# Backward pass of a cached-attention block: Wo times dao in batches, and another order of the first heads' work and transfers

## The chip, the cores and the metric

The kernel runs on one core of a Trainium2 chip. The metric is the device time of one execution in microseconds, given as the median of several runs. Engines are named as the profile names them: PE is TensorE (PEld its weight loads), DVE is VectorE, ACT is ScalarE, POOL is GpSimd, SP is SyncE, which here only issues DMAs.

## What is computed

A block with one query token (D = 640) and a cached attention of 32 heads, 8192 keys, head width 192, then a small mixer and MLP; the reference returns the output and the gradients of nine inputs. What matters here is the attention and its backward pass:

```python
q = (x @ wq)                       # 32 heads of 192
scores = einsum('bhqd,bhkd->bhqk', q, k) * Dh ** (-0.5)
p = softmax(scores)
o = einsum('bhqk,bhkd->bhqd', p, v)
a = o.reshape(B, Sq, Hq * Dh) @ wo
...
_out, _vjp = jax.vjp(_f, A_x, A_k_cache, A_v_cache, A_wq, A_wo, B_w3, B_w4, c, w_mod)
_grads = _vjp(grad_out)
```

For each head the backward pass needs, with dao the gradient of a (640 numbers) and P the softmax row: do = Wo·dao (192 numbers), dV = P ⊗ do, dP = V·do, c = do·o, dS = P·(dP - c), dK = dS ⊗ q, and dq from sums that the forward pass kept. K, V, dK and dV are each 100 MB in bf16 and go through HBM once, so 400 MB of the 569 MB that the kernel moves are these four.

## The kernel before

**Layout.** A head's K or V is 8192 rows of 192; a tile holds half a head, 128 partitions by 32 rows by 192 (128 x 6144 bf16, 1536 KB). Five such tiles ("big") serve the outputs dV and dK in the backward pass; six more slots (three in a pool "fv", three in "bv") form a ring for V.

**Order.** The forward pass takes heads 0 to 31 (to about 545 us), then the small mixer and its backward pass (to about 566 us), then the backward pass of the heads runs from 31 down to 0. The loop index i counts them: head HS[i] = 31 - i, and "nxt" is the head of i + 1. Iteration i computes dP, dS and dK of head i, and dV of head i + 1, so dV runs one head ahead. The first V tiles, both dV halves of head i = 0 and the first half of i = 1 are made ahead of the loop.

**One iteration of the loop** (lines 1235 to 1284), in program order:

1. On odd i, `bwd_dob` (L979): broadcasts do and q of the next pair of heads over all partitions, by matmuls with the identity (L191) that ScalarE copies out as do_pb and q_pb (L195).
2. `bwd_mult` (L996) for both halves t: VectorE multiplies V by do in place (`mul`, L132), and TensorE sums the product over groups of 8 columns into dP_ps by 24 accumulating matmuls (L1004). This frees the V slot.
3. `ring_load` (L749): issues the next transfers whose slot is free. A ring entry is half a V ("v", on SP's queue, L330) or a batch of Wo ("w", on POOL's queue, L764).
4. `bwd_pf` and `bwd_dv` (L1023) of the next head: ScalarE scales the first 20 rows of each half (L1009, one instruction a row), VectorE makes the other 12 (L987), and SP stores the half (L1012), which waits for both.
5. `hook` (L1188), in the first ten iterations: do of heads further on. Wo arrives as 15 pairs of heads in batches of three pairs (the last has two), one batch for two iterations. `bwd_ttr` (L920) multiplies one 640-wide row block of Wo by the broadcast dao and sums it, on VectorE, five and four blocks in the two iterations; then `fin_do`, `fin_c` (c = do·o, its sum on TensorE, L145) and `fin_dq_mm` (dq's matmuls, L950 to L953).
6. Store jobs: dwo (three ScalarE copies, L1054, stored from POOL's queue, L1073) and others.
7. `bwd_ds` (L1028): dP's last sum (L1030) and dS. For i = 0 then `dq_last` (L958), 128 small matmuls with K (L493, L496).
8. `bwd_dk` (L1035) for both halves: one VectorE product (L987) and one store on SP (L1039).

**What sets the order.** PE, DVE and ACT run in program order (`pin_order` at the end). SP and POOL carry only DMAs, in an order that the framework's scheduler gives them; each queue issues in that order, and an entry that waits holds those behind it. All big transfers, loads and stores, are on SP's queue.

The change touches `load_wo` (L761), `hook` (L1188), the tables ahead of it (L1176 to L1185) and the loop, and adds `bwd_wo_mult` and `bwd_wo_red` beside `bwd_ttr`.

Of the kernel before, what the change touches and what calls it, by code (L numbers as in the profile page):

```python
# [12 lines left out]
AX = mybir.AxisListType  # L13
# [7 lines left out]
def kernel(  # L21
# [43 lines left out]
    P = 128  # L65
# [62 lines left out]
    def ccol(n, name, dtype=FP32):  # L128
        return const.tile([P, n], dtype, name=name)

    def mul(out, a, b):
        nc.vector.tensor_tensor(out=out, in0=a, in1=b, op=ALU.mult)  # L132
# [600 lines left out]
    PS = list(range(HH - 1, -1, -1))  # L733
    V_b = {HS[0]: st[HS[0]]["V"], HS[1]: {1: st[HS[1]]["V"][1]}}
    wo_src = {(PS[k], cc): st[2 * PS[k] + 1]["wo"][:, cc, :] for k in range(2) for cc in range(3)}
    BATCHES = [(2, 3, 4), (5, 6, 7), (8, 9, 10), (11, 12, 13), (14, 15)]
    ring = []
    for i in range(1, HQ):
# [10 lines left out]
    def ring_load():  # L749
        while ring_n[0] < len(ring) and (ring_n[0] < 3 or ring_key(ring_n[0] - NR) in freed):  # L750
            n = ring_n[0]
            kind, k, t = ring[n]
            slot = ring_slot(n)
            pool = bv if slot > 2 else fv
            ring_n[0] += 1
            if kind == "v":
                V_b.setdefault(k, {})[t] = load_v(pool, k, t, slot, ldq if n >= 3 else nc.sync)
            else:
                load_wo(k, pool.tile([P, JH, DH], BF16, name="V_sb", tag=f"v{slot}"))

    def load_wo(k, tl):  # L761
        lo, n = PS[BATCHES[k][-1]], len(BATCHES[k])
        tl = tl.rearrange("p j d -> p (j d)")[:, 0 : 3 * n * D].rearrange("p (c r) -> p c r", r=D)
        nc.gpsimd.dma_start(out=tl, in_=wo_v[:, 3 * lo : 3 * (lo + n), :])  # L764
        for hp in range(lo, lo + n):
            for cc in range(3):
                wo_src[hp, cc] = tl[:, 3 * (hp - lo) + cc, :]

    def ring_key(n):
        return ring[n] if n >= 0 else (("v", HS[0], 0), ("v", HS[0], 1), ("v", HS[1], 1))[n]  # L770
# [144 lines left out]
    dmod_bf = ccol(NMC, "dmod_bf", BF16)  # L915

    dof = ccol(NQC, "dof")
    r3_all = ccol(NQC, "r3_all")

    def bwd_ttr(hp, cc):  # L920
        nc.vector.tensor_tensor_reduce(out=wo_src[hp, cc], in0=wo_src[hp, cc], in1=dao_bc, scale=1.0, scalar=0.0, op0=ALU.mult, op1=ALU.add, accum_out=dof[:, 3 * hp + cc : 3 * hp + cc + 1])  # L921

    def fin_do(lo, n):
        sl = slice(3 * lo, 3 * (lo + n))
        dve_copy(do_bf[:, sl], dof[:, sl])

    def fin_c(lo, n):
        sl = slice(3 * lo, 3 * (lo + n))
        dve_copy(do_f[:, sl], do_bf[:, sl])
        pc = bsm.tile([P, 9], FP32, name="pc")[:, 0 : 3 * n]  # L930
        mul(pc, do_f[:, sl], o_col_f[:, sl])
        pc2 = bsm.tile([P, 6], FP32, name="pc2")[:, 0 : 2 * n]
        stt(pc2[:, 0 : 2 * n : 2], pc[:, 1 : 3 * n : 3], mask_lo[:, 0:1], pc[:, 0 : 3 * n : 3], ALU.mult, ALU.add)
        stt(pc2[:, 1 : 2 * n : 2], pc[:, 1 : 3 * n : 3], mask_hi[:, 0:1], pc[:, 2 : 3 * n : 3], ALU.mult, ALU.add)
        return col_sums(pc2, 2 * n, "c_ps")
# [87 lines left out]
    def bwd_dv(h, t):  # L1023
        o = big_tile("dV")
        bwd_dv_act(o, h, t)
        bwd_dv_dve(o, h, t)
# [146 lines left out]
    J2[NPH + 8].append(job_x0)  # L1173
    J2[NPH + 14].append(job_c)

    ttrs = {i: [] for i in range(NPH)}  # L1176
    ttrs[0] = [(PS[1], cc) for cc in range(3)]
    fins = {}
    for b, ks in enumerate(BATCHES):
        units = [(PS[k], cc) for k in ks for cc in range(3)]  # L1180
        i = 1 + 2 * b
        ttrs[i] = units[0:5] if i + 1 < NPH else units
        if i + 1 < NPH:
            ttrs[i + 1] = units[5:]
        fins[min(i + 1, NPH - 1)] = (PS[ks[-1]], len(ks), b)  # L1185
    dq, cps = {}, {}

    def hook(i):  # L1188
        for u in ttrs[i]:
            bwd_ttr(*u)  # L1190
        if i == 0:
            fin_do(PS[1], 1)
            cps[i] = (PS[1], 1, fin_c(PS[1], 1))
        if i in fins:
            lo, n, b = fins[i]
            if b > 0:
                freed.add(("w", b, 0))
                ring_load()
            fin_do(lo, n)
            cps[i] = (lo, n, fin_c(lo, n))  # L1200
            dq[i] = (lo, n, fin_dq_mm(lo, n))
        if i == 3:
            dq[i] = (PS[1], 2, fin_dq_mm(PS[1], 2))
# [28 lines left out]
    bcast_dao()  # L1232
    mid_mm()
    AHEAD = 2 * NPH
    for i in range(HQ):
        h, nxt = HS[i], HS[i + 1] if i + 1 < HQ else None
        if i % 2 == 1 and nxt is not None:
            bwd_dob(nxt // 2)
        for f in J0[i]:
            f()  # L1240
        if i <= AHEAD:
            for t in range(2):
                bwd_mult(h, t, 2 if i == 0 else 1)
                if i == t == 0:
                    ring_load()
                    c_first = fin_c(PS[0], 1)
        ring_load()
        if i - 1 in dq:
            fin_dq(*dq.pop(i - 1))
        if i == 0:  # L1250
            fin_c_copy(PS[0], 1, c_first)
        if nxt is not None:
            if i > 0:
                bwd_pf(nxt)
            for t in range(0 if i > 0 else 1, 2):
                bwd_dv(nxt, t)
        if i < NPH:
            hook(i)
        if i == 3:
            bcast_cols(du_bf, 0, NFC, du_bc, act_copy)  # L1260
        for f in J1[i]:
            f()
        bwd_ds(h)
        if i == 0:
            dq_last(h)
        if i >= AHEAD and nxt is not None:
            for t in range(2):
                bwd_mult(nxt, t)
        bwd_dk(h, 0)
        bwd_dk(h, 1)  # L1270
        if i in cps:
            fin_c_copy(*cps.pop(i))
        if i == 1:
            mid_cols()
            job_mid()
            dve_copy(dmod_bf[:, 2 * NDC : 6 * NDC], dmod_c[:, 2 * NDC : 6 * NDC])
        if i == NPH - 1:
            fin_dq(*dq.pop(i))
            mm_cm.__exit__(None, None, None)
            for nm, b in (("in", 1), ("out", 4), ("bc", 1)):  # L1280
                side_cm.append(tc.tile_pool(name="side" + nm, bufs=b, side="right", reuse_waits="tile"))
                side[nm] = side_cm[-1].__enter__()
        for f in J2[i]:
            f()
        if i == I_SIDE:
            while side_cm:
                side_cm.pop().__exit__(None, None, None)
            xt = ctx.enter_context(tc.tile_pool(name="xt", bufs=1, side="right", reuse_waits="tile"))
            for k in "xy":
                tail_tiles[k] = (xt, "xt" + k)  # L1290
            for n in range(len(ring) - NR, len(ring)):
# [34 lines left out]
```

## Time and profile before

| | |
|---|---|
| median of 3 runs | 1381.43 us (1379.37 to 1382.59) |
| profiled execution | 1379.59 us, of which the span of instructions is 1377.8 us |
| DVE busy | 1070.5 us (78%) |
| ACT busy | 946.8 us (69%) |
| PE busy | 860.8 us (62%) |
| DMA | 569.26 MB, mean 413 GB/s; SP's queue 550.73 MB, POOL's 16.71 MB |
| V load (125 of them) | 1536 KB, 14.8 us from issue to landing (median) |
| dV store (61) and dK store (64) | 1536 KB each, 22.3 and 24.0 us |

How to read it: an engine's busy share is a mean over stages with different limits. "DMA share" is the mean busy share of the core's 16 DMA engines, so one engine alone is 0.06; it can read slightly over 1 because packets overlap by a few nanoseconds. "PEclk" is the granted share of TensorE's clock. In the view of stretches each row has the stretch, its length, then busy time and count of instructions for each engine, then the granted clock, the DMA share and the rate in GB/s. A row of the timeline has the start, the time, the engine, the line, the operation and the count of instructions merged into it.

### The profile page before, as it was taken

How to read it: one execution, taken by the hardware profiler on the slowest of the kernel's cores; microseconds unless marked ns; L12 is line 12 of the kernel's file. 1: busy time of each engine (PE TensorE's matmuls, PEld its weight loads, DVE VectorE, ACT ScalarE, POOL GpSimd, SP SyncE). 2: the span in 40 equal slices, each digit the busy share in tenths (PEclk: the TensorE clock that was granted, in tenths of full speed). 3: DMA queues.
4: the chain of work that ended last, by engine and by line, in shares of the span. 5: the costliest groups of instructions: out<-in, count | busy, mean ns of one | idle time of the engine just before them, and what ended most of it. 6: DMA issues, size and time to landing. Idle time of an engine off the chain costs nothing.

```text
span 1377.8 us, 28365 instructions
## 1 busy us (share of the span) xinstructions
PE 860.8 (62%) x11655; PEld 675.9 (49%) x11655; DVE 1070.5 (78%) x1273; ACT 946.8 (69%) x2586; POOL 21.5 (2%) x33
## 2 busy tenths in 40 slices
PE   3799999999999999748545653443344325324440
PEld 3577777777777777736434542322223223213330
DVE  3588787888788787899988986965868669679792
ACT  1388777887778785866676676766767676767770
POOL 0000000000000000000000000000000000000000
PEclk9899999999999999666666665666666767656665
DMA  9999999999999999899999999999999999999997
GB/s 392 416 417 418 420 418 421 414 419 418 405 421 419 403 420 387 337 367 413 419 418 419 427 429 425 425 427 423 426 426 423 428 422 415 425 425 422 428 428 319
DMA packets 71758, 569.26 MB, mean 413 GB/s; under 512 B 6796, under 2 KB 14476, under 8 KB 31436
## 3 DMA queue, kind: packets, MB, share of 16 engines
q1 hardware_dynamic: 67934, 550.73, 96.1%
q0 software_dynamic: 3664, 16.71, 3.0%
q8 instruction: 91, 1.49, 0.4%
q14 instruction: 39, 0.32, 0.1%
q10 hardware_dynamic: 30, 0.00, 0.0%
HBM read 341.51 MB, written 225.91 MB: 412 GB/s over the span
## 4 chain that ended last, share of the span: by engine, by line
DMA 37%; DVE 29%; PE 22%; ACT 6%; SPq 3%; issue 2%; DVEq 0%; ACTq 0%
DMA out_dram<-dV 24%; DVE prod L132 9%; PE ps_a L432 8%; DVE dK L987 5%; DVE V_sb L132 5%; DMA out_dram<-dK 4%; PE S_ps L372 4%; DMA V_sb<-in_A_v_cache_dram 3%; DMA K_sb<-in_A_k_cache_dram 3%; ACT dV L1009 3%; PE ps_b L443 3%; PE kb_ps L449 2%; DVE dV L987 2%; DVE V_sb L921 2%; DMA out_dram<-dw 2%
## 5 line engine op out<-in xcount | busy, mean ns | idle before, releaser
L1009 ACT ACTIVATE dV<-do_pb,PF 128x192 bf16<-128x192 bf16 x1246 | 435.8, 440 | 141.9 <-DMA out_dram<-dV 101.3
L1004 PE MATMUL dP_ps<-V_sb,ident_bf 128*128 128x256 bf16 (+1 forms) x1584 | 233.3, 322 | 212.0 <-DVE V_sb L132 212.0
L407 ACT ACTIVATE EK<-K_sb,E_f 128x192 bf16<-128x192 bf16 x992 | 351.1, 442 | 4.3 <-PE kb_ps L302 2.9
L1004 PEld LDWEIGHTS <-ident_bf 128*128 128x128 bf16 x1584 | 180.9, 117 | 264.2 <-issue 138.9
L987 DVE TENSOR_TENSOR dK<-dS,q_pb 128x6144 bf16<-128x6144 bf16 x64 | 212.9, 3354 | 26.2 <-DMA out_dram<-dK 15.6
L132 DVE TENSOR_TENSOR prod<-K_sb,q_pb 128x6144 bf16<-128x6144 bf16 x64 | 214.4, 3349 | 4.1 <-DMA K_sb<-in_A_k_cache_dram 4.1
L132 DVE TENSOR_TENSOR V_sb<-V_sb,do_pb 128x6144 bf16<-128x6144 bf16 (+1 forms) x66 | 212.0, 3253 | 0.0
L432 PE MATMUL ps_a<-EK,V_sb 128*128 128x193 bf16 x1984 | 195.1, 251 | 1.3 <-DMA V_sb<-in_A_v_cache_dram 1.3
L432 PEld LDWEIGHTS <-V_sb 128*128 128x128 bf16 x1984 | 167.8, 100 | 19.3 <-issue 12.7
L987 DVE TENSOR_TENSOR dV<-P2h,do_pb 128x2304 bf16<-128x2304 bf16 (+2 forms) x67 | 89.5, 1354 | 111.3 <-DMA out_dram<-dV 106.8
L414 DVE TENSOR_TENSOR EK<-K_sb,P2h 128x1536 bf16<-128x1536 bf16 x124 | 117.5, 948 | 0.0
L372 PE MATMUL S_ps<-prod,ident_bf 64*64 64x256 bf16 x3072 | 101.3, 280 | 11.5 <-DVE prod L132 11.5
L443 PE MATMUL ps_b<-EK,V_sb 128*64 128x193 bf16 x1984 | 107.7, 250 | 0.0
L372 PEld LDWEIGHTS <-ident_bf 64*64 64x64 bf16 x3072 | 86.5, 110 | 31.0 <-issue 26.9
L443 PEld LDWEIGHTS <-V_sb 128*64 128x64 bf16 x1984 | 80.8, 110 | 19.6 <-issue 15.9
L393 ACT ACTIVATE E_f<-sm_ps,negm 128x64 f32<-128x64 f32 x31 | 9.8, 315 | 103.9 <-DVE negm L391 103.9
L376 DVE TENSOR_REDUCE S<-S_ps 128x128 f32<-128x1024 f32 x32 | 39.2, 1224 | 47.7 <-PE S_ps L372 47.6
L1115 PEld LDWEIGHTS <-ident_bf 128*128 128x128 bf16 x112 | 15.2, 136 | 123.8 <-issue 122.9
L449 PE MATMUL kb_ps<-EK,hot_bf 128*32 128x384 bf16 x992 | 63.5, 333 | 0.0
L1115 PE MATMUL js_ps<-wq,ident_bf 128*128 128x480 bf16 x64 | 23.8, 557 | 53.3 <-DVE wq L132 53.3
L1115 PE MATMUL js_ps<-wm,ident_bf 128*128 128x400 bf16 x48 | 14.9, 494 | 48.7 <-DVE wm L132 48.7
L195 ACT CAST do_pb<-bc_ps 128x384 bf16<-128x384 f32 x15 | 7.1, 474 | 52.0 <-PE bc_ps L191 52.0
(259 smaller groups left out, 758.5 us busy)
## 6 DMA issues: line engine op xcount, KB each, us to landing
V_sb<-in_A_v_cache_dram SPq DMA_DIRECT2D x125, 1536.0 KB, 14.8
K_sb<-in_A_k_cache_dram SPq DMA_DIRECT2D x64, 1536.0 KB, 14.2
out_dram<-dK SPq DMA_DIRECT2D x64, 1536.0 KB, 24.0
out_dram<-dV SPq DMA_DIRECT2D x61, 1536.0 KB, 22.3
wq<-in_A_wq_dram SPq DMA_DIRECT2D x3, 2560.0 KB, 31.4
wo_t<-in_A_wo_dram SPq DMA_DIRECT2D x16, 480.0 KB, 14.3
out_dram<-dwo POOLq DMA_DIRECT2D x16, 480.0 KB, 8.9
wq<-in_A_wq_dram SPq DMA_DIRECT2D x4, 1920.0 KB, 23.7
```

The source lines that it names most:

```text
L132: nc.vector.tensor_tensor(out=out, in0=a, in1=b, op=ALU.mult)
L372: nc.tensor.matmul(st["S_ps"][c0 : c0 + 64, r, t * JH : (t + 1) * JH, :], lhsT=ident_bf[64 * r : 64 * r + 64, 64 * r : 64 * r + 64], rhs=p ...
L376: nc.vector.reduce_sum(out=st["S2"], in_=st["S_ps"], axis=AX.X)
L407: nc.scalar.activation(out=st["EK"][q][:, jj, 0:DH], in_=K_st[h, t][:, r * JQ + jj, :], func=ACT.Copy, scale=st["E_f"][:, j : j + 1])
L414: nc.vector.tensor_tensor(out=EK[:, NA:JQ, 0:DH].rearrange("p j (d r) -> p j d r", r=2), in0=K_st[h, t][:, r * JQ + NA : (r + 1) * JQ, :]. ...
L432: nc.tensor.matmul(st["A_ps"][:, 0:n], lhsT=V_sb[:, r * JQ + jj, a0:a1], rhs=EK[:, jj, 0:n], start=(q == 0 and jj == 0), stop=(q == 3 and ...
L443: nc.tensor.matmul(st["B_ps"][g : g + 64, 0:n], lhsT=V_sb[:, r * JQ + jj, b0:b1], rhs=EK[:, jj, 0:n], start=(q == 0 and jj < 2), stop=(q = ...
L449: nc.tensor.matmul(kb_ps[g : g + 32, 0 : 2 * DH], lhsT=hot_bf[:, HQ - 1 - h : 2 * HQ - 1 - h], rhs=EK[:, jj : jj + 2, 0:DH], start=(h == 0 ...
L987: nc.vector.tensor_tensor(out=o.rearrange("p j (d r) -> p j d r", r=2), in0=pairs[:, :, None, :].to_broadcast([P, n, NP2, 2]), in1=vec.rea ...
L1004: nc.tensor.matmul(bst[h]["dP_ps"][:, t * JH + r : t * JH + r + n, :], lhsT=ident_bf, rhs=V_sb[:, :, k * DS : (k + 1) * DS], start=(k == 0 ...
L1009: nc.scalar.activation(out=o[:, jj, :], in_=vec_of(do_pb, h), func=ACT.Copy, scale=bst[h]["PF"][:, t * JH + jj : t * JH + jj + 1])
L1115: nc.tensor.matmul(ps[:, 0 : NDC * W].rearrange("p (i w) -> p i w", w=W), lhsT=ident_bf, rhs=w[:, :, k * W : (k + 1) * W], start=(k == 0), ...
```

## The change

Four things, all in the first ten iterations of the loop:

- Wo times dao by batches: one product over a whole batch on VectorE (9 x 640 columns; 6 x 640 for the last) in odd iterations, whose sums TensorE takes by 20 accumulating matmuls with the identity into 32 columns a block; one VectorE reduction in the next iteration (the same one for the last batch) gives do.
- `bwd_dob` moves into the hook for i up to 8: behind `fin_do`, ahead of `fin_c` and of dq's matmuls. For i = 0, `bwd_ds` and `dq_last` go ahead of the hook.
- For i = 1 to 3, `bwd_pf` goes ahead of the V products and each dV half behind the V product of the same t.
- For i = 0 to 3, the second `ring_load` goes behind `bwd_dv`.

On the engines' queues this gives the following. SP, from the first V load of the loop on: before, V V dV dK dK, V dV dV dK dK, V V dV dV dK dK, V dV dV dK dK, dV dV V V V dK dK; after, V dV V dK dK, dV dV V dK dK, dV dV V V dK dK, dV dV V V dK dK, V V dV dV dK dK. On POOL the Wo load of the second batch stands behind the first store of dwo, before it stood ahead. PE gets 100 matmuls more; DVE loses 42 products with their 42 reads of the accumulator, and gets five products and five reductions.

```diff
+    def bwd_wo_mult(b):
+        lo, n = PS[BATCHES[b][-1]], len(BATCHES[b])
+        w = wo_b.pop(b)
+        mul(w, w, dao_bc[:, None, :].to_broadcast([P, 3 * n, D]))
+        ps = bank_s("dof_ps")[:, 0 : 3 * n * WS].rearrange("p (c w) -> p c w", w=WS)
+        for k in range(D // WS):
+            nc.tensor.matmul(ps, lhsT=ident_bf, rhs=w[:, :, k * WS : (k + 1) * WS], start=(k == 0), stop=(k == D // WS - 1))
+        dof_ps[b] = (ps, lo, n)
+
+    def bwd_wo_red(b):
+        ps, lo, n = dof_ps.pop(b)
+        nc.vector.reduce_sum(out=dof[:, 3 * lo : 3 * (lo + n)], in_=ps, axis=AX.X)
...
     def hook(i):
-        for u in ttrs[i]:
-            bwd_ttr(*u)
         if i == 0:
+            for u in wo_first:
+                bwd_ttr(*u)
             fin_do(PS[1], 1)
+            bwd_dob(PS[1])
             cps[i] = (PS[1], 1, fin_c(PS[1], 1))
-        if i in fins:
-            lo, n, b = fins[i]
+            return
+        if i % 2 == 1:
+            b = (i - 1) // 2
+            bwd_wo_mult(b)
             if b > 0:
                 freed.add(("w", b, 0))
                 ring_load()
+        if i in fins:
+            b = fins[i]
+            lo, n = PS[BATCHES[b][-1]], len(BATCHES[b])
+            bwd_wo_red(b)
             fin_do(lo, n)
+            if i % 2 == 0:
+                bwd_dob(HS[i + 2] // 2)
             cps[i] = (lo, n, fin_c(lo, n))
             dq[i] = (lo, n, fin_dq_mm(lo, n))
...
+    EARLY, SPLIT = range(4), range(1, 4)
     for i in range(HQ):
         h, nxt = HS[i], HS[i + 1] if i + 1 < HQ else None
-        if i % 2 == 1 and nxt is not None:
+        if i % 2 == 1 and i > NPH and nxt is not None:
             bwd_dob(nxt // 2)
...
         if i <= AHEAD:
+            if i in SPLIT:
+                bwd_pf(nxt)
             for t in range(2):
                 bwd_mult(h, t, 2 if i == 0 else 1)
                 if i == t == 0:
                     ring_load()
                     c_first = fin_c(PS[0], 1)
-        ring_load()
+                if i in SPLIT:
+                    bwd_dv(nxt, t)
+        if i not in EARLY:
+            ring_load()
...
-        if nxt is not None:
+        if nxt is not None and i not in SPLIT:
             if i > 0:
                 bwd_pf(nxt)
             for t in range(0 if i > 0 else 1, 2):
                 bwd_dv(nxt, t)
+        if i in EARLY:
+            ring_load()
+        if i == 0:
+            bwd_ds(h)
+            dq_last(h)
         if i < NPH:
             hook(i)
...
-        bwd_ds(h)
-        if i == 0:
-            dq_last(h)
+        if i > 0:
+            bwd_ds(h)
```

More of the change, by code (lines that the diff above doesn't have):

```diff
@@ L735 @@
     wo_src = {(PS[k], cc): st[2 * PS[k] + 1]["wo"][:, cc, :] for k in range(2) for cc in range(3)}
+    wo_b = {}
+    WS = 32
     BATCHES = [(2, 3, 4), (5, 6, 7), (8, 9, 10), (11, 12, 13), (14, 15)]
@@ L763, in load_wo @@
         tl = tl.rearrange("p j d -> p (j d)")[:, 0 : 3 * n * D].rearrange("p (c r) -> p c r", r=D)
+        wo_b[k] = tl
         nc.gpsimd.dma_start(out=tl, in_=wo_v[:, 3 * lo : 3 * (lo + n), :])
-        for hp in range(lo, lo + n):
-            for cc in range(3):
-                wo_src[hp, cc] = tl[:, 3 * (hp - lo) + cc, :]
     def ring_key(n):
@@ L917 @@
     dof = ccol(NQC, "dof")
+    dof_ps = {}
     r3_all = ccol(NQC, "r3_all")
@@ L1174 @@
     J2[NPH + 14].append(job_c)
[L1176 to L1185, printed above, removed]
+    wo_first = [(PS[1], cc) for cc in range(3)]
+    fins = {min(2 + 2 * b, NPH - 1): b for b in range(len(BATCHES))}
     dq, cps = {}, {}
     def hook(i):
-        for u in ttrs[i]:
-            bwd_ttr(*u)
         if i == 0:
+            for u in wo_first:
+                bwd_ttr(*u)
             fin_do(PS[1], 1)
+            bwd_dob(PS[1])
             cps[i] = (PS[1], 1, fin_c(PS[1], 1))
-        if i in fins:
-            lo, n, b = fins[i]
+            return
+        if i % 2 == 1:
+            b = (i - 1) // 2
+            bwd_wo_mult(b)
             if b > 0:
```

## The prediction

> **What bounds the kernel now.** First the page: the strip of DMA shares and rates, and the chain of work that ended last.
>
> ```profile
> span 1377.8 us, 28365 instructions
> ...
> DMA  9999999999999999899999999999999999999997
> GB/s 392 416 417 418 420 418 421 414 419 418 405 421 419 403 420 387 337 367 413 419 418 419 427 429 425 425 427 423 426 426 423 428 422 415 425 425 422 428 428 319
> ...
> DMA 37%; DVE 29%; PE 22%; ACT 6%; SPq 3%; issue 2%; DVEq 0%; ACTq 0%
> ```
>
> A slice is 34.4 us. The sixteen DMA engines move above 400 GB/s nearly everywhere; slices 16 to 18 (516 to 620 us) drop to 387, 337, 367. The change touches only what starts at 575 us. So I cut that region into short stretches (the view of busy time by stretches; the last two columns are DMA share and GB/s).
>
> ```profile
> core 0: us, PE busy (x) PEld busy (x) DVE busy (x) ACT busy (x) POOL busy (x), PEclk, DMA share, GB/s
> 580.00:582.00 2.00, 2.00 (x36) 2.00 (x35) 2.00 (x2) 2.00 (x7) 0.00 (x0) 0.97 0.76 300
> 582.00:584.00 2.00, 2.00 (x38) 1.98 (x36) 2.00 (x3) 2.00 (x7) 0.00 (x0) 1.00 0.83 206
> ...
> 588.00:592.00 4.00, 3.67 (x122) 3.56 (x121) 3.97 (x3) 0.00 (x0) 0.00 (x0) 0.50 1.00 329
> 592.00:602.00 10.00, 4.79 (x37) 3.42 (x35) 9.90 (x6) 8.68 (x25) 0.00 (x0) 0.50 1.01 427
> 602.00:603.00 1.00, 1.00 (x6) 0.71 (x5) 1.00 (x1) 1.00 (x4) 0.00 (x0) 0.50 0.53 221
> 603.00:604.00 1.00, 1.00 (x7) 0.73 (x5) 1.00 (x2) 1.00 (x4) 0.00 (x0) 0.50 0.14 41
> 604.00:605.00 1.00, 1.00 (x11) 0.87 (x10) 1.00 (x2) 1.00 (x4) 0.00 (x0) 0.99 0.99 160
> 605.00:606.00 1.00, 1.00 (x11) 0.90 (x10) 1.00 (x5) 1.00 (x5) 0.00 (x0) 1.00 0.43 135
> ...
> 612.00:1360.00 748.00, 325.53 (x1992) 245.59 (x1992) 593.68 (x503) 507.40 (x1318) 17.44 (x22) 0.65 1.01 424
> 1360.00:1368.00 8.00, 0.00 (x0) 0.00 (x0) 0.00 (x0) 0.00 (x0) 0.00 (x0) 0.50 0.95 404
> 1368.00:1372.00 4.00, 0.00 (x0) 0.00 (x0) 0.00 (x0) 0.00 (x0) 0.00 (x0) 0.50 0.29 123
> 1372.00:1376.00 4.00, 0.00 (x0) 0.00 (x0) 0.00 (x0) 0.00 (x0) 0.00 (x0) 0.50 0.06 28
> ```
>
> From 612 to 1360 us the share is 1.01: no engine's work there is worth anything, only bytes are. What can be won lies before 612: the hole from 602 to 606, (0.47 + 0.86 + 0.01 + 0.57) = 1.9 us by share, and by bytes against 427 GB/s (206 + 386 + 267 + 292 KB) / 427 = 2.7 us, since a queue that restarts is slow; and 580 to 584 (0.8 us by share). What was late for the hole? SP's queue, in order of time:
>
> ```profile
> 581.43 3.27 SPq L330 DMA_DIRECT2D V_sb<-in_A_v_cache_dram  x2
> 585.44 0.34 SPq L1012 DMA_DIRECT2D out_dram<-dV  x1
> 591.75 3.60 SPq L1039 DMA_DIRECT2D out_dram<-dK  x2
> 603.68 0.34 SPq L330 DMA_DIRECT2D V_sb<-in_A_v_cache_dram  x1
> 604.12 4.69 SPq L1012 DMA_DIRECT2D out_dram<-dV  x2
> ```
>
> Nothing is issued from 595.4 to 603.68. Then comes a V load, held by TensorE's last read of its slot, and behind it the first dV half of the head, although VectorE had finished that half at 603.1. A transfer is 1.57 MB, 3.7 us at 427 GB/s.
>
> **The change, part by part** (i is the loop's index, times those of this profile).
>
> *i = 0, the hole.* VectorE is unchanged up to the dV half that ends at 584.03. dP's sum, now next, waits for TensorE's last product (584.35): 0.68 + 0.35, dS at 585.45 instead of 588.3. Three Wo products (0.74 apart, 2.3) and the small do and c steps (586.38 to 587.34, 0.95) follow: 588.7. Two dK (6.63): 595.3, 0.3 later than now. dq_last's matmuls (588.38 to 592.2, 3.8) now run from 585.45 to 589.3, then the broadcasts (0.48): do_pb cast at 590.3, q_pb 590.9, PF 591.2. ScalarE starts dV at 591.2 instead of 594.5; twenty rows take 7.0: halves done at 598.2 and 605.2 instead of 601.5 and 608.5.
>
> *i = 1.* VectorE: P2h 0.2, V product 3.3, dV part 1.3: the first half is whole at 600.2 (now issued at 604.1). Product and part again: 604.85; ScalarE's 605.2 ends the second (now 608.48). Behind it, SP's V load goes at 605.6 (now 603.68) and needs nothing by then: V is used three heads later. DMA is busy with dK until about 602.7, the first half carries it to 606.4, and the second, issued at 605.2, comes 1.0 to 1.3 us later (the issue at 603.68 shows in the row from 604): 606.2 to 606.5. The hole shrinks to 0.1 at most; 0.3 is kept for it. What is late next is ScalarE's second half.
>
> *Gain:* 1.9 to 2.7 less 0.3: 1.6 to 2.4, taken at 2.0, the middle.
>
> *Price in i = 0:* the second V load now stands behind the dV store, which waits for ScalarE until 585.42: V, dV, V, dK in place of V, V, dV, dK, two turns more between reading and writing. No row shows such a turn alone. Above: the stretch 588 to 592, where one falls, 329 GB/s at full share, (98 x 4) / 427 = 0.9 us each; below: nothing, as over 612 to 1360, with turns in every head. I take 0.25 each, nearer to the long row, since the load is issued with another transfer ahead of it: 0.5; range 0 to 1.8.
>
> *Wo by batches, heads 1 to 9.*
>
> ```profile
> L132 DVE TENSOR_TENSOR V_sb<-V_sb,do_pb 128x6144 bf16<-128x6144 bf16 x22 | 72.8, 3350 | 0.0
> L921 DVE CUSTOM_DVE_ANT_0 V_sb<-V_sb,dao_bc 128x640 bf16<-128x640 bf16 x42 | 32.0, 819 | 0.0
> L1030 DVE TENSOR_REDUCE dP<-dP_ps 128x64 f32<-128x512 f32 x12 | 8.2, 688 | 0.2
> ```
>
> 42 products go, 0.744 apart (five from 604.38 to 608.10): 31.3 us. Four of 5760 columns and one of 3840 come, by the first row (two in 6.54) 3.07 and 2.04: 14.3; five sums of 288 or fewer columns, by the third row 0.39: 1.9. VectorE saves 15.1 us, worth nothing while the share is 1.01; without that cover it is a rival below. TensorE gets 100 matmuls of up to 288 columns: 24 of 256 took 5.3 us at clock 0.50 (598.37 to 603.67) and 2.9 at 1.00 (to 606.53), so twenty take 2.7 to 5.0. Behind them stand the small output's transposes, dq's matmuls and the next head's products, which wait for two dK and a V product (9.9 us): hidden. A V load of i = 3 waits for them, some 50 us ahead of its use. Their sums take one of the two PSUM banks that dP uses, which the head before has left.
>
> *Broadcasts ahead of dq's matmuls* (8.5 us, 632.65 to 641.2): ScalarE's wait of 10.1 us before 641.74 goes. dV halves are ready earlier; the share is 1.01: nothing. By the same steps the stores of heads 2 and 3 are issued at 623.4, 628.0, 642.9 and 648.3, with work queued until about 629, 634, 650 and 654: no new hole, the nearest being 6 us away.
>
> *POOL:* the first Wo load now stands behind dwo's store of i = 1, which waits for ScalarE: about 609 instead of 606.83; used at 648, free.
>
> **Sum:** 2.0 - 0.5 = 1.5 us less. The profiled execution took 1379.59 (span 1377.8 and 1.8 around it), 1.8 under the median, 1381.43, of runs from 1379.37 to 1382.59: 1378.1 on its scale, **1379.9** on the median's.
>
> **The rivals.**
>
> *More comes back* (1376.9). If a fuller queue also spares the slow stretches, 580 to 584 by bytes 1.6 us, 588 to 592 0.9, and the hole whole 2.7, against 0.7 of costs: 4.5 less. For it: rates under 380 at full share occur only where the queue is short. Against: 580 to 584 lies ahead of anything moved.
>
> *VectorE is the bound.* The chain of waits runs along VectorE from 568 to 675. Heads 1 to 4 lose 18 products (13.4) for two batch products and two sums (6.9): 6.5 less, 1374.9. Against: DMA's share, 1.01 all through.
>
> *The slowest DMA engine sets the end* (1380.9). From 1372 to 1376 the share is 0.06, one of sixteen; at 603 it is 0.14, two still at work. If the engine that ends last was one of those, it lost about 1 us in the hole, not 2.0, so 1.0 of the 1.5 goes: 0.5 is left. [...]
>
> *SP's order costs more than it brings* (1384.6). SP issues in order, so whatever delays a dV half delays the V load and the dK behind it. If ScalarE's dV start stays at 594.5 (broadcasts no earlier), the second half is issued at 608.5: DMA idles from 606.4 to 609.7, 3.3 instead of 1.9, and the turns at their upper price add 1.8: 3.2 slower on balance. It decides from 605.2 on: each us later is one lost. For it: three waits in a row (ScalarE, V, dK) on one queue. Against: dq_last's start follows dS by the rows.
>
> **How the numbers follow.** Forecast 0.38, slowest engine 0.09: within 0.2% (2.8 us, about what a measurement of this kernel can tell from no change): 0.47. More comes back 0.28, VectorE 0.05: faster 0.33. SP's order 0.20: slower. The forecast's own bounds are 2.4 less (no price) to 0.2 more (1.6 less 1.8). For 8 in 10 the range takes in the first rival and the near half of the last, and leaves out VectorE's and the far half: 1376.5 to 1384.8.
>
> **What would show it.** Right: no stretch under a share of 0.8 after 590; the first dV store of i = 1 near 600 and the second near 605; dS of i = 0 near 585.4; the rest of the span at 1.01 and shorter by the hole. Wrong: a hole at 606 to 610 (ScalarE's halves late), new dips where V loads alternate with stores, a share below 1 after 612, or a rate over 612 to the end that differs from 424 GB/s; 1 GB/s there is 1.8 us, as much as the whole forecast.

## The result, and the profile after

The changed kernel takes 1377.33 us (median of 14 runs, 1376.61 to 1380.06). The kernel before, run beside it, takes 1380.16 (14 runs, 1379.36 to 1382.59). The ratio is 0.9979, 95% interval 0.9972 to 0.9986: 2.8 us less, between 1.9 and 3.9.

The profiled execution of the changed kernel is the slowest of its 14 (1380.06, span 1378.3), so its span must not be set against before's 1377.8. Its unchanged forward part ran late: the first dV store is issued at 570.97 us, 568.67 before. I count from that store below, as +t. From it to the end of the span is 809.1 us before and 807.3 after, 1.8 less. Set against one profile, a number after is read 2.3 earlier.

The changed kernel's page: span, strip and chain of work that ended last:

```profile
span 1378.3 us, 28492 instructions
...
DMA  9999999999999999899999999999999999999997
GB/s 393 415 416 420 418 418 420 421 413 421 416 407 420 417 419 362 318 394 425 422 419 427 423 427 423 421 428 422 424 425 422 427 420 417 425 425 420 428 427 316
...
DMA 43%; DVE 25%; PE 21%; ACT 5%; issue 2%; SPq 1%; DVEq 0%; ACTq 0%
```

Slices 16 and 17 (516 to 585 us) look worse than before (362 and 318 against 387 and 337), because the unchanged part ahead of the loop ran late in them and the first hole, at 580 to 588 us, is larger; slice 18 is better, 394 against 367. In the chain, DMA rose from 37 to 43% and VectorE fell from 29 to 25%. A strip of 34 us is too coarse for the rest. The same kernel by stretches (busy us of PE, PEld, DVE, ACT, POOL, then TensorE's granted clock, DMA share, GB/s):

```profile
582.00:584.00 2.00, 2.00 (x21) 2.00 (x20) 2.00 (x2) 2.00 (x7) 0.00 (x0) 0.50 0.91 362
584.00:586.00 2.00, 2.00 (x32) 2.00 (x30) 2.00 (x3) 2.00 (x7) 0.00 (x0) 0.83 0.45 89
586.00:588.00 2.00, 1.66 (x30) 1.54 (x28) 0.74 (x2) 1.71 (x5) 0.00 (x0) 1.00 0.71 270
588.00:592.00 4.00, 3.17 (x110) 3.10 (x110) 3.83 (x14) 0.00 (x0) 0.00 (x0) 0.94 1.01 393
592.00:602.00 10.00, 1.87 (x32) 1.54 (x29) 10.00 (x6) 8.97 (x26) 0.00 (x0) 0.50 1.01 426
602.00:603.00 1.00, 0.94 (x5) 0.68 (x5) 1.00 (x2) 1.00 (x4) 0.00 (x0) 0.50 1.01 430
603.00:604.00 1.00, 1.00 (x7) 0.67 (x6) 1.00 (x2) 1.00 (x4) 0.00 (x0) 0.50 0.98 418
604.00:605.00 1.00, 1.00 (x7) 0.67 (x6) 1.00 (x1) 1.00 (x4) 0.00 (x0) 0.50 0.98 418
605.00:606.00 1.00, 1.00 (x10) 0.86 (x9) 1.00 (x1) 1.00 (x4) 0.00 (x0) 0.91 1.02 430
606.00:608.00 2.00, 1.75 (x17) 1.42 (x15) 2.00 (x3) 2.00 (x7) 0.00 (x0) 1.00 1.04 442
608.00:612.00 4.00, 2.44 (x22) 1.94 (x20) 3.93 (x4) 3.31 (x8) 1.45 (x2) 1.00 1.03 403
612.00:614.00 2.00, 1.54 (x13) 0.98 (x11) 2.00 (x1) 2.00 (x7) 0.36 (x1) 1.00 0.95 264
614.00:616.00 2.00, 0.00 (x0) 0.00 (x0) 2.00 (x2) 2.00 (x7) 0.00 (x0) 1.00 0.97 375
616.00:618.00 2.00, 0.00 (x0) 0.00 (x0) 2.00 (x1) 2.00 (x7) 0.00 (x0) 1.00 0.97 349
...
612.00:1360.00 748.00, 335.50 (x2085) 254.40 (x2083) 582.12 (x438) 505.92 (x1316) 17.81 (x23) 0.68 1.01 423
...
1372.00:1376.00 4.00, 0.00 (x0) 0.00 (x0) 0.00 (x0) 0.00 (x0) 0.00 (x0) 0.50 0.06 28
```

The second hole (602 to 606 before, shares 0.53, 0.14, 0.99, 0.43) is gone: no stretch from 588 to 612 is under 0.98. Between +22 and +45 the DMA engines idle 0.09 us of their time, before 2.10. The first hole has grown: 2.0 us idle between +8 and +22, 1.0 before. Behind the place of the second hole, from 612 to 618, the share is 0.95 to 0.97 but the rate only 264 to 375 GB/s: SP issues nothing between 608.9 and 615.3, and the short queue moves less. From 612 to 1360 the share is 1.01 as before. The rate there is 423 after 424, which the prediction named as a sign of being wrong; this window now takes in the slow 612 to 618, and the count of bytes below shows 0.4 us lost from +45 to +60 and none over the rest (2.2 us ahead at +45, 2.0 at +780). SP's queue shows the new order that filled the second hole:

```profile
584.78 0.34 SPq L330 DMA_DIRECT2D V_sb<-in_A_v_cache_dram  x1
587.74 0.33 SPq L1026 DMA_DIRECT2D out_dram<-dV  x1
588.16 0.38 SPq L330 DMA_DIRECT2D V_sb<-in_A_v_cache_dram  x1
595.29 3.60 SPq L1053 DMA_DIRECT2D out_dram<-dK  x2
603.33 5.09 SPq L1026 DMA_DIRECT2D out_dram<-dV  x2
608.52 0.39 SPq L330 DMA_DIRECT2D V_sb<-in_A_v_cache_dram  x1
```

The first dV half of i = 1 goes at 603.33, while the last dK (issued at 598.56) is still moving until 607.4; the second (608.09) comes before the first has landed (609.3, the median of this transfer's sixteen parts, which land from 609.0 to 611.0).

The first hole grew for a reason that the change does not touch. The 48 matmuls of the first two V products begin at 579.5 at a clock of 0.50 and take 5.28 us (4.24 before, where the clock was 0.97 from 580). The first V load, which waits for TensorE's sums of its slot, goes out at 584.78, +13.8 instead of +12.8.

### The profile page after: what moved, and what is told of

It reads as the page before. It is cut to its first block, busy times and chain, and to the rows that moved or that the text cites. A ratio compares the mean times of both kernels' runs of the same rounds, so it can differ in the third digit from the quotient of the medians.

```text
span 1378.3 us, 28492 instructions
## 1 busy us (share of the span) xinstructions
PE 874.9 (63%) x11755; PEld 687.6 (50%) x11755; DVE 1055.2 (77%) x1199; ACT 946.0 (69%) x2586; POOL 21.5 (2%) x33
## 4 chain that ended last, share of the span: by engine, by line
DMA 43%; DVE 25%; PE 21%; ACT 5%; issue 2%; SPq 1%; DVEq 0%; ACTq 0%
DMA out_dram<-dV 24%; DMA K_sb<-in_A_k_cache_dram 8%; DVE prod L132 8%; DMA out_dram<-dK 7%; PE ps_a L432 7%; DVE dK L1001 6%; DVE V_sb L132 5%; PE S_ps L372 4%; ACT EK L407 3%; PE ps_b L443 2%; PE dP_ps L1018 2%; PE kb_ps L449 2%; DVE dV L1001 2%; DMA V_sb<-in_A_v_cache_dram 2%; ACT dV L1023 2%; DMA out_dram<-dw 2%
## 5 line engine op out<-in xcount | busy, mean ns | idle before, releaser
L1068 ACT ACTIVATE dwo<-dao_bc,o_col_f 128x640 bf16<-128x640 bf16 x48 | 36.1, 816 | 0.0
```

## The experiments

All kernels were timed in five rounds beside the kernel before; the ratios carry about 0.0009 (1.2 us) either way, as much as many of the effects. So I also read each trace by the bytes that its DMAs still have to move at +t, less the same in the profile of before, divided by 424 GB/s (worked out from the packets): how many us of transfer a kernel is ahead (minus) or behind. (V is moved twice: its 125 loads make 197 MB, so K, V, dK and dV are some 499 of the 569 MB.) This is one profile each; it shows where a difference arises, and the ratios show what comes of it.

| kernel | ratio [95%] | us | idle, +22 to +45 | bytes at +30 | +45 | +60 | +75 | +120 | +780 |
|---|---|---|---|---|---|---|---|---|---|
| changed | 0.9979 [0.9972, 0.9986] | -2.9 | 0.09 | 0.4 | -2.2 | -1.8 | -2.8 | -3.2 | -2.0 |
| e1 order only | 0.9989 [0.9980, 0.9998] | -1.5 | 0.14 | -0.2 | -2.7 | -2.5 | -3.2 | -2.9 | -2.1 |
| e2 batches only | 0.9990 [0.9981, 0.9999] | -1.4 | 2.28 | -0.2 | 0.0 | 0.0 | -0.5 | -0.2 | 0.3 |
| e3 late broadcast | 0.9990 [0.9981, 0.9998] | -1.4 | 2.86 | -0.2 | 0.6 | 0.6 | -0.4 | -0.7 | 0.8 |
| e4 V loads first | 1.0003 [0.9994, 1.0012] | 0.4 | 2.31 | 0.0 | 0.3 | 0.3 | -0.3 | -0.4 | -0.1 |
| e5 TensorE warm | 0.9980 [0.9971, 0.9989] | -2.8 | 0.06 | -0.1 | -3.0 | -2.8 | -3.8 | -3.9 | -3.0 |
| e6 no Wo products | 1.0029 [1.0017, 1.0040] | 4.0 | 0.13 | 0.0 | -2.5 | -2.3 | -3.2 | -0.2 | 5.5 |
| e7 turns | 0.9987 [0.9979, 0.9996] | -1.8 | 0.01 | 0.3 | -2.8 | -1.8 | -2.8 | -3.2 | -2.3 |
| e8 two heads | 0.9992 [0.9983, 1.0001] | -1.1 | 0.10 | 0.2 | -2.4 | -1.4 | -1.0 | -1.3 | -1.5 |
| e9 no Wo, early copy | 0.9982 [0.9974, 0.9991] | -2.5 | 0.12 | -0.2 | -2.8 | -2.6 | -3.5 | -3.7 | -3.6 |
| e10 heads 2, 3 | 1.0000 [0.9991, 1.0009] | 0.0 | 1.16 | 0.7 | -0.3 | -0.3 | -1.2 | -1.6 | -0.7 |
| e11 warm, before | 1.0005 [0.9996, 1.0014] | 0.7 | 1.41 | -0.3 | -1.0 | -1.0 | -0.5 | -0.9 | 0.1 |
| e12 before, no Wo | 1.0007 [0.9997, 1.0016] | 1.0 | 0.74 | 0.5 | -1.2 | -1.2 | -2.1 | -1.7 | -0.2 |

("us" is the ratio less 1, times 1380.)

My theory after the result: the new order of transfers and dV halves fills the hole at the end of i = 0, and nothing else in the change matters. Rivals: VectorE's relief by the batches; the order in later heads.

**e1, the order without the batches.**

```diff
-            bwd_wo_mult(b)
+            for u in units((i - 1) // 2)[0 : 5 if i + 1 < NPH else None]:
+                bwd_ttr(*u)
...
-            bwd_wo_red(b)
+            if i % 2 == 0:
+                for u in units(b)[5:]:
+                    bwd_ttr(*u)
```

> The whole new order, with Wo times dao left as 45 single products on VectorE. Theory 'hole' (the gain of 2.8 us is the DMA idle time at 602 to 606 us, closed by the order of the first two heads; VectorE's 15 us are worth nothing under a full DMA queue): the same gain as the whole change, 2 to 3 us under before, about 1377.4, and no DMA idle time between the dK stores of i = 0 and the dV stores of i = 1. Theory 'VectorE' (the batches bring it): no gain, about 1380.

The slot of a Wo batch is freed in the even iteration again, as in the kernel before. The idle time at the hole (0.14) and the lead in bytes are the changed kernel's. By time it has only half of the gain, -1.5; its interval (-2.8 to -0.3) overlaps the changed kernel's.

**e2, the batches without the order** (loop, hook and SP's order as before).

```diff
-    EARLY, SPLIT = range(4), range(1, 4)
...
-            bwd_dob(PS[1])
...
-        if i == 0:
-            bwd_ds(h)
-            dq_last(h)
         if i < NPH:
             hook(i)
```

> Wo times dao by batches alone, in the old order. Theory 'hole': the batch of i = 1 comes after the hole, so it stays as it was, about 2 us of DMA idle time; 0 to 0.5 us under before, about 1380. Theory 'VectorE': the gain is here, 2 to 6 us, 1374 to 1378.

The hole stays (2.28) and the bytes at +45 are those of before, but the time is 1.4 less. Trace and time disagree here. Taken alone, e1 and e2 would also fit a gain that is half the order's and half the batches'. Against that, e4 and e10 below have the batches without the new order of i = 0 and 1 and are at +0.4 and 0.0; e9 and e12 ask what VectorE's time is worth.

**e3, broadcasts and hook back in their old place, dV halves and loads as changed.**

```diff
-            bwd_dob(PS[1])
...
-        if i % 2 == 1 and i > NPH and nxt is not None:
+        if i % 2 == 1 and (i == 1 or i > NPH) and nxt is not None:
...
+        if i < NPH:
+            hook(i)
         if i == 0:
             bwd_ds(h)
             dq_last(h)
-        if i < NPH:
-            hook(i)
```

> The changed kernel, but in i = 0 dP's sum, dS and dq's matmuls stand behind the hook again and the broadcasts of do and q come at the start of i = 1, so that ScalarE starts its dV rows some 2 to 3 us later. Theory 'hole' in the form of the ledger (each us that the second dV half of i = 1 is late is a us of DMA idle time): an idle stretch of about 2 to 3 us ahead of that half, and the gain gone, 1379 to 1381. Theory 'queue' (what counts is that the dV stores stand ahead of the V load on SP, and the DMA queue has slack): gain kept, about 1377.5.

This kernel brings about the recorded rival "SP's order costs more". ScalarE is late, and SP's queue and the stretches of e3 show what follows:

```profile
601.83 7.25 SPq L1026 DMA_DIRECT2D out_dram<-dV  x2
609.17 0.38 SPq L330 DMA_DIRECT2D V_sb<-in_A_v_cache_dram  x1
```

```profile
604.00:606.00 2.00, 2.00 (x17) 1.62 (x15) 2.00 (x2) 2.00 (x7) 0.00 (x0) 0.82 1.08 449
606.00:608.00 2.00, 1.41 (x13) 1.08 (x12) 2.00 (x2) 2.00 (x7) 0.63 (x1) 1.00 0.24 94
608.00:610.00 2.00, 2.00 (x19) 1.56 (x16) 1.93 (x3) 2.00 (x5) 0.38 (x1) 1.00 0.46 54
```

The hole has moved to 606 to 610, between the two halves, and is larger (2.86), as that rival had it. The V load, free earlier, stands behind the late half. Yet the time is 1.4 under before. In e2 and e3 the time goes against the hole, and I have no cause. Their profiles show the slowest of their eleven executions (1380.92 against a median of 1378.61, and 1380.22 against 1378.84), so they need not show what the others did.

**e4, loads and dV halves as before, broadcasts early.**

```diff
-    EARLY, SPLIT = range(4), range(1, 4)
+    EARLY, SPLIT = range(0), range(0)
```

> The changed kernel, but V loads ahead of dV again in heads 0 to 3 and both V products ahead of both dV halves; batches, early dS and early broadcasts stay. Theory 'hole': VectorE finishes the first dV half of i = 1 some 3 us later and SP holds it behind the V load: the hole is back, 1.5 to 2.5 us idle, and 0 to 1 us under before, about 1379.7. Theory 'broadcasts' (the earlier start of ScalarE is what counts): gain kept, about 1377.5.

The hole is whole (2.31), and the time is before's within 1.2 us. Early broadcasts and batches together show no gain while the first dV half stands behind the V load on SP's queue.

**e5, the changed kernel with TensorE kept busy ahead of the loop**, so that the first V products run at full clock.

```diff
+    warm_ps = bank("k", name="warm_ps")
+    for _ in range(10):
+        nc.tensor.matmul(warm_ps, lhsT=ident_bf, rhs=dbo_bc[:, 0:512], start=True, stop=True)
```

> The changed kernel with ten products of the identity with 512 columns of a broadcast row put on TensorE behind the mixer's matmuls, so that it is busy ahead of the loop's first V products (nothing reads them). In the changed kernel those 48 products ran at a clock of 0.50 in 5.28 us and the first V load of the loop waited for the last of them; in the kernel before they ran in 4.24. Theory that the holes are what is to be won (DMA is full elsewhere): the first V load goes out 1 to 2 us earlier, the first hole (580 to 588 us, 2.0 us idle in the changed kernel) shrinks to about 1, and the time is 1 to 2 us under the changed kernel's 1377.3, so 1375.3 to 1376.3. Rival, that something else than TensorE (the dV halves made by ScalarE and VectorE) holds that hole: no change, 1377.3. If the ten products themselves delay the loop by more than the clock gives: up to 2 us more, 1379.

Its stretches:

```profile
582.00:584.00 2.00, 1.83 (x31) 1.71 (x31) 2.00 (x3) 2.00 (x7) 0.00 (x0) 1.00 1.02 295
584.00:586.00 2.00, 1.14 (x21) 1.02 (x19) 1.71 (x3) 2.00 (x7) 0.00 (x0) 1.00 1.00 406
586.00:588.00 2.00, 1.69 (x60) 1.65 (x60) 2.00 (x6) 0.24 (x1) 0.00 (x0) 1.00 0.82 344
```

The clock is 1.00 and the first hole is 0.33 us instead of 2.0; the bytes are 0.8 further ahead at +45, and 1.0 at +780. e11 shows the same in the old order (0.23 us instead of 1.0, at a clock of 1.00): in both orders the hole is smaller where TensorE's clock is up at the first V products. Ahead of them the ten products ran in 572 to 576 us (PE busy 3.67 of 4, clock 0.61), behind a PE busy all of 568 to 572 at 0.50; from 576 on the clock was 1.00. How much work brings it up is not shown. The ratio is the changed kernel's (0.9980 against 0.9979), so of the 1 to 2 us expected none is seen by time, with 1.2 us of uncertainty in each ratio.

**e11, the same ten products in the kernel before.**

> The kernel before with the ten products of e5 on TensorE behind the mixer's matmuls, nothing else. Theory that TensorE's clock at the first V products sets the first hole (580 to 588 us): in the profile of before these ran partly at clock 1.00 by luck (4.24 us against 5.28), so this gives 0.5 to 1 us in the hole's size and the time is 0.5 to 1 us under before; the second hole (602 to 606 us) stays. Rival, that the warm-up only helps with the changed order: no difference.

The first hole shrinks here too (0.23 us idle instead of 1.0), the second stays, smaller (1.41), and by +75 half of the lead is lost; the time is not under before's. That the first hole is worth its 1 us is not shown by time in either kernel. The edit is e5's three lines, at the same place.

**e6, the changed kernel without the products of Wo and their sums** (do of later heads is a copy of a column of Wo).

```diff
-        mul(w, w, dao_bc[:, None, :].to_broadcast([P, 3 * n, D]))
-        ps = bank_s("dof_ps")[:, 0 : 3 * n * WS].rearrange("p (c w) -> p c w", w=WS)
-        for k in range(D // WS):
-            nc.tensor.matmul(ps, ...)
-        dof_ps[b] = (ps, lo, n)
+        dof_ps[b] = (w, lo, n)
...
-        nc.vector.reduce_sum(out=dof[:, 3 * lo : 3 * (lo + n)], in_=ps, axis=AX.X)
+        dve_copy(dof[:, 3 * lo : 3 * (lo + n)], ps[:, :, 0])
```

> The changed kernel with the batch products of Wo with dao and TensorE's sums of them left out (do of the later heads is then a copy of one column of Wo, so what the rest computes is not the gradient; all transfers stay). VectorE loses another 14.3 us of products, as much again as the change saved, TensorE 100 matmuls. Theory that DMA's share of 1.01 makes VectorE's time worthless: within 0.5 us of the changed kernel, 1377.3. Theory that part of the gain comes from VectorE's relief in heads 1 to 9: 2 us or more below it, 1375 or less.

Neither theory: 4.0 us slower than before with less to do. SP's queue, its longest waits and the stretches of e6:

```profile
646.56 0.33 SPq L1022 DMA_DIRECT2D out_dram<-dV  x1
646.98 20.30 SPq L330 DMA_DIRECT2D V_sb<-in_A_v_cache_dram  x2
667.34 0.90 SPq L1049 DMA_DIRECT2D out_dram<-dK  x2
```

```profile
SPq L330 <- DVE do_bf L198: 19.3, 1, 19.3
```

```profile
660.00:664.00 4.00, 4.00 (x25) 2.97 (x24) 3.89 (x13) 4.00 (x13) 0.00 (x0) 0.62 1.02 412
664.00:668.00 4.00, 3.00 (x31) 2.56 (x28) 3.80 (x11) 4.00 (x13) 0.00 (x0) 1.00 0.71 265
```

My edit had a side effect: the copy reads the Wo batch an iteration later than the product did, while the loads keep their places on SP. The next V load wants the slot of that batch, waits 19.3 us, and two finished dK halves stand behind it on SP. What is queued lasts until about 664 us; then DMA idles. This comes back at 720 and 772 us. Idle time after +45 is 4.1 us, 0.1 in the changed kernel. It is a clean picture of how SP's order turns one late read into lost time: 19.3 us of waiting on the queue, 4.1 us of idle DMA engines.

**e9, the same without the side effect** (the copy where the product stood).

```diff
+        dve_copy(dof[:, 3 * lo : 3 * (lo + n)], w[:, :, 0])
+        dof_ps[b] = (lo, n)
```

> The changed kernel with the batch products of Wo with dao and TensorE's sums of them left out, do of the later heads being a copy of one column of Wo (so the rest computes other numbers than the gradient; all transfers stay). Unlike the run before it, the copy is made where the product stood, so that the slot of the batch comes free as early as in the changed kernel or earlier. Theory that the run before it was slow because SP's queue waited for the late copy (a V load issued at 666.95 us behind 646.98), not for want of products: the holes at 664 to 672, 720 to 724 and 760 to 780 us go, and with DMA full the time is within 0.5 us of the changed kernel's 1377.3. Rival, VectorE's 16 us matter: 1375 or less. Rival, leaving the products out slows the kernel by itself: 1380 or more.

The holes go and the time is the changed kernel's (0.9982 against 0.9979), though VectorE's busy time from 612 to 1360 us is 15 us less (567.0 in the row below, 582.1 in the changed kernel):

```profile
612.00:1360.00 748.00, 326.74 (x1992) 247.02 (x1992) 566.97 (x433) 503.79 (x1310) 17.44 (x22) 0.66 1.01 424
```

**e12, the kernel before without its 42 products.**

```diff
+    def bwd_take(hp, cc):
+        dve_copy(dof[:, 3 * hp + cc : 3 * hp + cc + 1], wo_src[hp, cc][:, 0:1])
...
         for u in ttrs[i]:
-            bwd_ttr(*u)
+            if i == 0:
+                bwd_ttr(*u)
+            else:
+                bwd_take(*u)
```

> The kernel before, with the 42 products of Wo with dao after the first iteration left out: a copy of one element a partition takes the place of each (do of the later heads is then another number than the gradient's; all transfers and SP's order stay as before). VectorE loses about 28 us of the 31 that these products take, twice what the batches save. Theory that DMA's share of 1.01 makes VectorE's time worthless outside the hole: 0 to 1.2 us under before, the upper end if the five products ahead of the second dV half at 608 us held it (its store went out at 608.48). Rival, the reading of e2's time (1.4 us under before) as VectorE's relief: twice that, 2.8 us under before.

VectorE is busy 1041.5 us instead of 1070.5, and the time is not below before's (the interval is -0.4 to +2.2 us). With e9, no gain from VectorE's relief shows with the old order or the new, and in the old order more than 0.4 us is excluded. e2's -1.4 is then no relief of VectorE; what it is stays open, chance among it (its interval reaches to -0.1).

The second hole is smaller here (0.74) although SP's order is that of before, and the traces show why. The V load on which the dV halves of i = 1 wait stands behind 24 products of TensorE. In before, e2 and e4 the clock is 0.50 nearly to their end (0.50 in 602 to 604 us for before and e2, 0.57 for e4), and the hole is 2.10 to 2.31; in e10, e11 and e12 it has risen (1.00, 0.91 and 0.88 there), the load goes at +34.1 to +34.7 instead of +35.0 to +35.2, and the hole is 0.74 to 1.41. (In e10 and e12 the first hole is larger, 1.4 to 1.5, so that what is queued also lasts longer.) So with the old order the second hole is 1.7 on the mean of six profiles, and before's profile has one of the large ones.

**e7, V V dV in i = 0 again**, to take the two added turns away.

```diff
-    EARLY, SPLIT = range(4), range(1, 4)
+    EARLY, SPLIT = range(1, 4), range(1, 4)
```

> The changed kernel, but in the first iteration the second V load goes out ahead of the dV store again (V, V, dV, dK, dK instead of V, dV, V, dK, dK); the rest as changed. The recorded price of the two added turns between reading and writing: this one is 0.5 us faster, 1376.8. The reading after the result, that a V load right behind another V load is the slow one (4.58 us of service against 3.45 behind a dV store): 0.6 us slower, 1377.9, which shows in the trace as a service of 8.2 us for the second V and the dV store together instead of 7.5. The time alone cannot tell these apart; the services can.

From one transfer's median landing to the next, the second V load and the dV store take together, with V V dV, 4.58 + 3.68 = 8.3 us before, 8.1 to 8.4 in e2, e4, e7, e10 and e12, and 8.7 in e11. With V dV V they take 3.97 + 3.45 = 7.4 in the changed kernel, 7.5 to 7.8 in e1, e3, e6, e8 and e9, and 4.87 + 3.99 = 8.9 in e5, where the store was issued only 0.98 us before the V load ahead of it had landed (3.2 in the changed kernel). So two more turns cost nothing visible where work is queued, and the slow transfer of 588 to 592 was the second of two V loads in a row. Two in a row are not slow by themselves: in the later heads of before, where such a load was issued more than 8 us ahead of the landing of the one in front of it and POOL moved nothing, it takes 3.7 us (median of 15). In i = 0, where it is issued only 2.1 to 3.2 us ahead, it takes 4.4 to 5.0, and a dV store issued like that 4.0 to 4.3: the short queue goes with most of the loss, V behind V with the rest. By the bytes at +45 (e7 -2.8, changed -2.2) and by time (e7 1.1 us slower, within the intervals) no price and no gain is sure.

**e8, the new order in i = 0 and 1 only; e10, in i = 2 and 3 only.**

```diff
-    EARLY, SPLIT = range(4), range(1, 4)
+    EARLY, SPLIT = range(2), range(1, 2)            # e8
+    EARLY, SPLIT = range(2, 4), range(2, 4)         # e10
```

> The changed kernel with the new order of loads and dV halves only in the first two iterations (i = 0 and 1); iterations 2 and 3 have the order of before. Hole theory: all that the order brings lies in the hole at the end of i = 0, so the time is the changed kernel's, 1377.3, and the share after 612 us stays at 1.01. Rival, that the order in heads 2 and 3 brings a part (a higher rate there by turns that cost less): about 0.5 to 1 us slower, 1378 or so.

> The changed kernel with the new order of loads and dV halves only in iterations 2 and 3; in the first two the order of before (dV behind both V products, second V load ahead of it). Theory formed from the bytes still to be moved in the other runs: the order brings about 1.8 us in the hole at the end of the first iteration and another 1.0 to 1.5 us between 628 and 645 us, in iteration 2, where two V loads in a row meet a nearly empty queue; then this kernel has the hole (2 us idle between 600 and 610), gets the second part, and is 1.0 to 1.5 us faster than before. Recorded theory that only the hole can be won: as before with batches, 0.2 to 0.5 us faster, and no difference in bytes across 628 to 645 us.

e8 has filled the hole (0.10), but loses 1.4 us of its lead between +45 and +75. The stretches there, of before, of the changed kernel, and of e8:

```profile
625.00:630.00 5.00, 5.00 (x35) 3.86 (x34) 4.97 (x9) 5.00 (x14) 0.00 (x0) 0.71 1.04 415
630.00:635.00 5.00, 3.04 (x25) 2.64 (x22) 4.79 (x12) 1.60 (x3) 0.77 (x1) 0.97 0.98 391
635.00:640.00 5.00, 5.00 (x26) 4.82 (x25) 5.00 (x4) 0.00 (x0) 0.00 (x0) 0.50 1.00 381
```

```profile
625.00:630.00 5.00, 4.83 (x27) 3.59 (x28) 5.00 (x4) 0.07 (x1) 0.00 (x0) 0.59 1.02 417
630.00:635.00 5.00, 4.60 (x43) 4.09 (x41) 4.57 (x10) 2.31 (x5) 0.00 (x0) 1.00 1.01 425
635.00:640.00 5.00, 5.00 (x30) 4.79 (x29) 5.00 (x2) 4.97 (x14) 0.79 (x1) 0.59 1.01 427
```

```profile
625.00:630.00 5.00, 5.00 (x44) 4.12 (x42) 4.83 (x11) 0.12 (x1) 0.00 (x0) 0.89 1.00 362
630.00:635.00 5.00, 4.60 (x31) 4.39 (x30) 4.93 (x4) 4.97 (x12) 0.79 (x1) 0.79 1.03 401
635.00:640.00 5.00, 4.10 (x22) 3.97 (x22) 5.00 (x3) 5.00 (x16) 0.00 (x0) 0.50 0.95 351
```

Look at the last two columns: the share is near 1 in all three, the rate is not. Where i = 2 begins with two V loads issued only when the last dK is landing (the first 0.98 us ahead of that landing in e8, 2.8 before), the DMA engines are busy but move less; with a dV store first, issued 3.8 us ahead, they move 425. Before, 630 to 640 loses (36 + 46) x 5 / 427 = 0.96 us. e10 keeps the hole (1.16) and gains 0.9 in bytes between +60 and +75, as the changed kernel does (1.0), but its time is before's; e8's time says that this part is worth 1.8. The two times contradict each other, and the bytes of e12, with the old order, gain 0.9 there as well. So this second part is seen in rates; its size in time is open, somewhere from 0 to 1.8 us.

**All together.** The six kernels that fill the second hole with the order of i = 0 and 1 (changed, e1, e5, e7, e8, e9) average (2.9 + 1.5 + 2.8 + 1.8 + 1.1 + 2.5) / 6 = 2.1 us under before; the five that leave that order as it was (e2, e4, e10, e11, e12) average 0.1 over. If the intervals of 1.2 us are independent, the difference of 2.2 is sure to about 0.7. (e3 and e6 are in neither group: e3 has the order and a hole, e6 lost 4.1 us elsewhere. Within e1 to e4 alone, which were timed together, the times do not separate them: e1 is at -1.5, e2 and e3 at -1.4.) By bytes the six gain 1.6 to 2.7 us from +30 to +60, mean 2.2; against the mean of the five and before it is 1.7, because in three of the five the hole was smaller than in before's profile. Counted in the profiles from the first dV store to the end of the span, the six take 805.5 to 807.7 us and the five, before and e3 808.4 to 811.2, without overlap; e2 (808.9) and e3 (809.5) lie with the kernels that keep a hole. No kernel is shown to be faster than the changed one.

## Why the prediction was right, and where it was not

- *What bounds the kernel.* Right: e9 and e12 take 15 and 29 us from VectorE and show no gain, while closing the hole does.
- *Gain by the hole: 2.0, from 1.6 to 2.4.* Right in mechanism: 2.10 us idle became 0.09. The size fits, since kernels with and without the hole differ by 2.2, but there is luck in it: the prediction took the hole of one profile, and with the old order it is 0.74 to 2.31, small where TensorE's clock rose early. Its steps came 0.6 to 1.0 late (after, less 2.3): dS done at 586.5 for 585.45, ScalarE's dV start 591.8 for 591.2, the first half's store 601.0 for 600.2, the second 605.8 for 605.2, the V load 606.2 for 605.6. The delay arises in the first step, where VectorE waited 1.26 us for TensorE, which had done the first V products at half clock:

```profile
587.70 0.69 DVE L1044 TENSOR_REDUCE dP<-dP_ps 128x64 f32<-128x512 f32 x1 [1.26 <-PE dP_ps L1018]
588.42 0.35 DVE L141 SCALAR_TENSOR_TENSOR dS<-dP,c_bc,P2h 128x128 bf16<-128x128 f32 x1
```

 The prediction took the clock of one execution as given. It did no harm because the queue ran later too: the first half landed at 607.0 on that scale, not 606.4, still 1.2 us after the second was issued.
- *Price of two turns: 0.5, from 0 to 1.8.* Wrong: the mis-sized term. It was read from 588 to 592 (329 GB/s), which is the second of two V loads in a row, not a turn. No such price shows: e7, without the turns, is not faster, and by the landings V dV V takes less (7.4 to 7.8 us) than V V dV (8.1 to 8.4) where the second transfer was issued 2.2 to 3.2 us ahead.
- *Later heads: "the share is 1.01: nothing".* The step that failed. A share of 1 was taken as a full rate; the rates of 391 and 381 at 630 to 640 us were in the trace of before and were not used. The new order raised them to 425 and 427, up to 0.9 us by bytes, which the times neither confirm nor exclude (e8 and e10). Hole 2.0, this stretch 0 to 0.9 and no price make 2.0 to 2.9; measured 2.8, from 1.9 to 3.9. How the 2.8 divides between the two is open.
- *Batches.* Right: five products of 3.15 and 2.15 us (3.07 and 2.04 predicted), sums of 0.45 (0.39), twenty matmuls in some 2.6 us from 610.93 (2.7 to 5.0); VectorE's busy time fell by 15.3 us (15.1), and no gain from it shows.

```profile
L132 DVE TENSOR_TENSOR V_sb<-V_sb,dao_bc x5: 2150/3150/3151, 607.7 to 797.7; 128x5760 bf16<-128x5760 bf16 x4, 128x3840 bf16<-128x3840 bf16 x1
```

- *The number.* 1379.9 was set on the 1381.43 of three runs; 14 runs put before at 1380.16. Of the 2.6 us that it missed, 1.3 is this base and 1.3 the size (1.5 forecast, 2.8 measured). The size lies outside the forecast's own bounds (2.4 less to 0.2 more), though its interval does not. The range held it, near its low end, because it had been widened for the rival "More comes back".
- *Rivals.* "More comes back" (4.5 less) had the right idea, rates below 427 at full share where the queue is short. Its "only" does not hold: from 744 to 748 us before reads 368 GB/s at a share of 1.00 with four transfers of 1.57 MB issued on SP's queue and not yet landed, and a Wo load just issued on POOL's. Of its places, the hole came back; 588 to 592 gained some 0.8 us by the landings (8.3 to 7.4), though not in e5 (8.9); 580 to 584 did not gain, and the stretch of i = 2 was not among them. "VectorE" falls by e9 and e12. "The slowest DMA engine" is not borne out: the last engine works alone for 4.5 us before and 4.7 after, so it got what the hole gave. "SP's order" did not come true, but e3 and e6 show that both its mechanisms exist.

## What to carry to other kernels

When DMA is full nearly everywhere, look for the few us where its queue runs dry and ask which instruction the next transfer in the in-order queue waited for; here, moving that transfer behind one that is ready was worth more than 29 us off an engine that does not set the end. Look at more than one profile before sizing such a hole: with the same order it was 0.74 us in one and 2.31 in another. Read rate as well as share: where the queue was short, before moved 329 GB/s at a share of 1.00 (588 to 592 us), against 424 at 1.01 over the long stretch. And any edit that reads a buffer later, even by a cheap copy, can stop such a queue for everything behind it, as in e6 (19.3 us).

## What the runs showed that was not expected

- In i = 0, a 1.57 MB V load right behind another and issued 2.1 to 3.2 us before that one has landed takes 4.4 to 5.0 us from landing to landing, a dV store issued like that 4.0 to 4.3, at a DMA share near 1 in both; 3.7 at 427 GB/s, and 3.7 for a V load behind another where the queue is long. A dV half behind another, issued 1.1 to 1.9 us before that one had landed, takes 4.4 to 4.8 us (seven kernels, i = 1). Over the long stretch from 612 to 1360 us, with reads and writes mixed, the DMA engines move 423 to 424 GB/s at a share of 1.01; single rows of 2 us read up to 449, at a share of 1.08 (e3, 604 to 606).
- TensorE's clock at one place, ahead of anything changed, differed between the profiles of before and after (0.97 and 0.50 in 580 to 582 us, the same 48 products 4.24 and 5.28 us), and the first hole with it (1.0 and 2.0 us); at the 24 products ahead of the second hole, an earlier rise goes with 0.7 to 1.4 us idle instead of 2.1 to 2.3.
- In both kernels one DMA engine of sixteen still has about ten packets of 0.46 us when the others are done: 4.5 to 4.7 us at a share of 0.06, more than this change is worth.
